# Two-head state matmuls, and a third of one product's transposes moved from TensorE to the sync queue's DMA

## The chip, the cores and the metric

The kernel runs on one core of a Trainium2 chip. A core has engines that run beside each other, each through its own instructions in order: TensorE (PE, matmuls; the profile shows its weight loads apart as PEld), VectorE (DVE), ScalarE (ACT), GpSimd (POOL) and SyncE (SP), which here issues transfers only. Matmul results land in PSUM; the other data lies in SBUF. Sixteen DMA engines move data. The metric is device microseconds (us) of one execution.

## The reference

The inputs r, k, v, w have 4 batches, 8 heads, 768 steps and 48 elements. For each batch and head a recurrence with a 48x48 state runs over the steps:

```python
cur   = einsum(u * k_t, v_t)              # outer product, weighted by u
y_t   = einsum(r_t, state + cur)
state = w_t[:, None] * state + einsum(k_t, v_t)
```

The rows y (3072 rows of 8 x 48 = 384) then go through a mixture of low-rank adapters: eight gate logits by a 384x8 matrix, the two largest kept, softmax over these, and

```python
delta[mask] += weight * ((x[mask] @ A[e]) @ B[e])   # A: 384x16, B: 16x384, 8 adapters
out = x + delta
```

## The kernel before

The 3072 rows are cut into 24 tiles of 128 steps; six tiles (one batch) form a sequence, after which the state begins anew (`t % 6 == 0`). Within a tile the recurrence is done by matmuls, and between tiles by a state that TensorE accumulates.

The stages of one tile `t`, with the line of the profile at which each shows:

- `ln` (L324/L326, ACT): logarithm of w. `cs` (L333, L334, PE) sums it over the steps into `cs_ps`; `grow` (L346, ACT) is its exponential; `ci` (L351, PE) adds the tile's own step, `exps` (L356, ACT) is the inverse exponential. `mult` (L362, DVE) multiplies r and k with these into `rk2`, whose head slots are 64 wide (48 used).
- `tr` (L404, PE) transposes `rk2` in eight pieces, `trev` moves the result to SBUF (ACT at L206 or DVE at L208). `amm` (L442, PE) forms the scores of the eight heads, `aev` (L453, DVE) masks them.
- `rkp` (L379, POOL) is the plain product r*k. For the diagonal term, the sum over u*r*k, it must be transposed: `xk` (L538, PE) transposes three blocks of `rkp` of the tile LEAD = 3 ahead together with three blocks of its own result `xs`, and `xkev` (L206/L208, ACT or DVE) moves all six to SBUF. `dgmm` (L383, PE) multiplies by u, `dgev` (L200/L202) moves the sums of two tiles at a time, and `dv` (L396, POOL) multiplies v by them.
- `kv` (L475, PE) adds the tile's k x v to the state in PSUM: eight matmuls, one for each head, into the diagonal blocks `S_acc[g*64:..., p, g]`. A zeroing matmul (L471) stands ahead of a sequence's first and in the last tile. `sev` (L200 on ACT, L202 on DVE) copies the state to SBUF. The off-diagonal blocks are zero, as only the zeroing matmul writes them.
- `yi` (L498, PE; not in a sequence's first tile) multiplies r by the copied state of the tile before, in four matmuls for two heads each, of 96 columns: so the off-diagonal blocks must be zero. `ya` (L524, PE) adds scores times v. `xev` (L529, DVE) adds `dv`: the result `xs`.
- The adapters: `lgmm` (L559, PE) the logits; then for batches of 4, 4, 4, 4, 4, 2, 1 and 1 tiles `gate` (L566), `gmax` (L573), `gden` (L579, L580), `gsel` (L592/L589), `gmul` (L599, L600, POOL), `zmm` (L607, PE), `zw` (L614, DVE), `zT` (L624, PE), `zTev`. `dmm` (L640, PE) is the second adapter matrix. The last addition `oev` is either on DVE (L651), or on ACT (L649) after an identity matmul (L639, PE) that adds `xs` in PSUM; tiles 22 and 23 use L646 on DVE. `store` (L655, SP) writes the tile.

Loads: w on SP (`load_w`, L255); r and k together, cast to 16 bits on the way by POOL's queue (`load_rk`, L264; the first four tiles plain on SP, L261); v likewise (`load_v`, L276 and L272).

The order of the work is a list written out, `ORDER`: items such as `xk.12` are emitted one after the other, and each engine (SP's and POOL's queues among them) runs its own in that order. An item starts when its engine has come to it, its inputs are there, and its buffer is free. `ENGINES` names for each stage the tiles that go to ACT ('A') or DVE ('D'). Where a product on POOL (`rkp`, `dv`) follows a multiply on DVE in the list, a wait keeps it behind that multiply. `rkp` has three buffers, `S_sb` three, `res` sixteen.

Of the kernel before, what the change touches and what calls it, by code (L numbers as in the profile page):

```python
# [55 lines left out]
ENGINES = {'out': {0: 'A', 3: 'A', 8: 'A', 12: 'A', 13: 'A', 15: 'A', 16: 'A', 18: 'A', 20: 'A', 21: 'A', 17: 'A'},
    'k_id16': {0: 'A'}, 'trev': {0: 'D', 5: 'D', 9: 'D'}, 'xkev': {-3: 'D', -2: 'D'}, 'sev': {0: 'D'}, 'dgev': {1:
    'D', 5: 'D'}, 'cast_v': {1: 'D'}, 'cast_b': {0: 'D'}, 'zTev': {3: 'A', 7: 'A', 11: 'A', 15: 'A', 19: 'A', 21: 'A',
    22: 'A', 23: 'A'}}
# [5 lines left out]
m_zeros.0 load_w.0 load_w.1 szero.0 warm.0 warm.1 warm.2 ln.0 load_rk.0 k_incl.0 k_ident.0 k_strict.0 k_id16.0 warm.3
load_w.2 m_pad.2 cs.0 m_pad.0 grow.0 ln.1 multr.0 k_rest.0 load_rk.1 csx.0 exps.0 multk.0 rkp.0 warm.4 load_rk.4 ci.0
cs.1 warm.5 m_pad.1 m_pad.3 warm.6 warm.7 warm.8 grow.1 ci.1 exps.1 tr.0 trev.0 ln.2 load_v.0 xk.-3 load_v.2 xkev.-3
warm.9 cs.2 grow.2 amm.0 load_rk.6 rkp.1 cast_v.0 ci.2 exps.2 mult.1 tr.1 load_rk.2 rkp.2 trev.1 warm.10 cs.3 xk.-2
load_k.0 aev.0 cast_k.0 load_w.4 grow.3 xkev.-2 ln.4 amm.1 ya.0 dgmm.0 xk.-1 warm.11 load_v.4 dgmm.1 ci.3 exps.3
load_rk.3 mult.2 load_v.6 tr.2 load_v.1 cs.4 xkev.-1 dgev.1 dv.0 kv.0 trev.2 aev.1 mult.3 load_rk.8 sev.0 grow.4 xev.0  # L70
load_v.8 amm.2 rkp.3 ci.4 exps.4 cast_v.1 tr.3 load_w.6 mult.4 aev.2 yi.1 cs.5 dv.1 xk.0 trev.3 grow.5 xkev.0 kv.1
ci.5 ya.1 dgmm.2 ln.6 exps.5 lgmm.0 tr.4 dgmm.3 sev.1 rkp.4 amm.3 xev.1 dgev.3 dv.2 dv.3 rkp.5 load_rk.10 trev.4
mult.5 cs.6 xk.1 kv.2 yi.2 aev.3 load_w.8 tr.5 grow.6 sev.2 xkev.1 ci.6 exps.6 trev.5 ln.8 ya.2 kv.3 amm.4 xev.2 rkp.6
mult.6 dgmm.4 cs.7 yi.3 lgmm.1 ya.3 grow.7 xev.3 xk.2 ci.7 sev.3 tr.6 yi.4 aev.4 exps.7 xkev.2 xk.3 cs.8 dgmm.5 kv.4
xkev.3 mult.7 amm.5 grow.8 dgev.5 aev.5 lgmm.2 trev.6 lgmm.3 gate.3 ci.8 gmax.3 gsel.3 load_rk.12 gden.3 zmm.3 exps.8
sev.4 load_v.12 ya.4 cs.9 tr.7 rkp.7 load_b.0 dv.4 xev.4 gmul.3 load_w.10 kv.6 ln.10 grow.9 trev.7 zw.3 dv.5 amm.6
ci.9 dgmm.6 yi.5 xk.4 zT.3 exps.9 sev.6 cast_b.0 xkev.4 mult.8 cs.10 rkp.8 aev.6 mult.9 zTev.3 kv.7 ya.5 dgmm.7
grow.10 sev.7 dgev.7 tr.8 dmm.2 ci.10 trev.8 ya.6 load_w.12 amm.7 kv.8 xev.5 xk.5 exps.10 cs.11 tr.9 sev.8 xkev.5 yi.7
oev.2 lgmm.4 aev.7 yi.8 grow.11 ln.12 dv.6 dv.7 xev.6 ci.11 dgmm.8 store.2 rkp.9 mult.10 kv.9 exps.11 xk.6 ya.7
load_w.14 cs.12 amm.8 trev.9 xkev.6 dgmm.9 dmm.0 grow.12 dgev.9 xev.7 aev.8 ci.12 sev.9 rkp.10 exps.12 xk.7 xkev.7  # L80
tr.10 trev.10 dv.8 lgmm.6 load_rk.14 cs.13 mult.11 mult.12 rkp.11 ya.8 xev.8 oev.0 kv.10 grow.13 amm.9 aev.9 tr.11
ln.14 ci.13 lgmm.5 dgmm.10 dv.9 load_rk.16 lgmm.7 dmm.1 xk.8 gate.7 exps.13 load_w.16 oev.1 xkev.8 gmax.7 trev.11
load_rk.18 mult.13 amm.10 yi.9 cs.14 gsel.7 grow.14 dgmm.11 zmm.7 dgev.11 gden.7 aev.10 tr.12 ci.14 ya.9 sev.10 kv.12
gmul.7 zw.7 amm.11 dv.10 yi.10 ya.10 rkp.12 zT.7 trev.12 exps.14 cs.15 load_w.18 xev.9 ln.16 xk.9 aev.11 zTev.7 dv.11
rkp.13 sev.12 grow.15 yi.11 tr.13 ya.11 ci.15 xkev.9 trev.13 xev.10 mult.14 load_v.16 rkp.15 rkp.14 amm.12 kv.13 xk.10
dmm.4 exps.15 xev.11 sev.13 xkev.10 aev.12 cs.16 lgmm.8 tr.14 dgmm.12 dmm.5 dmm.7 lgmm.10 dgmm.13 grow.16 oev.4
trev.14 ci.16 mult.15 dgev.13 exps.16 ln.18 load_rk.20 oev.7 oev.5 dv.12 dmm.3 kv.14 amm.13 aev.13 rkp.17 xk.11 ya.12
sev.14 cs.17 xkev.11 xev.12 load_w.20 grow.17 tr.15 dgmm.14 lgmm.9 amm.14 kv.15 dv.13 oev.3 mult.16 ci.17 aev.14
trev.15 exps.17 rkp.16 xk.12 dmm.6 yi.13 lgmm.11 ya.13 mult.17 cs.18 xev.13 rkp.18 gate.11 xkev.12 tr.16 dgmm.15
grow.18 oev.6 gmax.11 amm.15 lgmm.12 trev.16 ci.18 dgev.15 dv.14 xk.13 exps.18 xkev.13 aev.15 yi.14 tr.17 ya.14 cs.19  # L90
store.3 yi.15 amm.16 zmm.11 sev.15 gsel.11 grow.19 trev.17 xev.14 ci.19 mult.18 xk.14 ln.20 tr.18 dgmm.16 ya.15
gden.11 load_w.22 exps.19 cs.20 xkev.14 dgmm.17 gmul.11 dv.15 dgev.17 yi.16 aev.16 load_rk.22 grow.20 trev.18 ya.16
mult.19 zw.11 kv.16 amm.17 store.1 zT.11 xev.15 ci.20 xk.15 dv.16 load_v.20 sev.16 exps.20 tr.19 cs.21 aev.17 rkp.19
zTev.11 xkev.15 grow.21 xev.16 dmm.8 dmm.11 amm.18 oev.8 mult.20 oev.11 lgmm.15 xk.16 yi.17 lgmm.13 lgmm.14 trev.19
gate.15 ci.21 dmm.9 ya.17 store.0 store.6 aev.18 gmax.15 kv.18 dv.17 xkev.16 xev.17 exps.21 amm.19 gsel.15 rkp.20
ln.22 ya.18 gden.15 oev.9 dgmm.19 dgmm.18 xk.17 store.7 store.4 store.5 dgev.19 sev.18 cs.22 gmul.15 xkev.17 dv.18
tr.20 grow.22 aev.19 zmm.15 yi.19 trev.20 lgmm.17 ci.22 ya.19 dv.19 rkp.21 exps.22 kv.19 xev.18 zw.15 sev.19 amm.20
store.11 store.8 zT.15 xev.19 cs.23 zTev.15 mult.21 dmm.10 store.9 dmm.13 rkp.22 oev.13 aev.20 xk.18 xkev.18 dgmm.20
tr.21 trev.21 xk.19 lgmm.16 mult.22 dmm.14 dgmm.21 oev.10 kv.20 xkev.19 rkp.23 dgev.21 amm.21 dmm.12 dv.20 lgmm.18
lgmm.19 yi.20 oev.14 grow.23 sev.20 gate.19 store.10 store.14 oev.12 aev.21 ya.20 dmm.15 ci.23 tr.22 exps.23 trev.22  # L100
gmax.19 yi.21 xev.20 gden.19 ya.21 xk.20 kv.21 dv.21 amm.22 mult.23 tr.23 store.13 store.12 oev.15 xkev.20 sev.21
gsel.19 zmm.19 gmul.19 trev.23 xev.21 store.15 dgmm.23 dgmm.22 xk.21 dgev.23 aev.22 xkev.21 amm.23 kv.22 sev.22 zw.19
zT.19 dv.22 yi.22 ya.22 dv.23 zTev.19 aev.23 xev.22 lgmm.20 lgmm.21 dmm.17 yi.23 ya.23 gate.21 gmax.21 oev.17 store.17
xk.22 xev.23 dmm.18 xkev.22 gsel.21 oev.18 dmm.19 zmm.21 gden.21 kv.23 lgmm.22 store.18 oev.19 store.19 xk.23 gmul.21
# [29 lines left out]
def kernel(  # L134
# [47 lines left out]
    Ss = [const.tile([128, P, 2, D], BF16, name=f"S_{i}") for i in range(S_BUFS)] if KV128 else []  # L182
    rk2s = [const.tile([L, 2, P, 2, 64], BF16, name=f"rk2_{i}") for i in range(NRK)]

    cs_ps = pp.tile([L, 512], F32, name="cs_ps")
# [305 lines left out]
        copy(engine("sev", t), sb, S_acc)  # L491
        st[t]["S"] = sb

    def yi(t):
        d = st[t]
        y_ps = pp.tile([L, H, D], F32, name="y_ps", **slot("y", t))
        for p in range(P):
            nc.tensor.matmul(y_ps[:, 2 * p:2 * p + 2, :].rearrange("s a b -> s (a b)"),  # L498
                             lhsT=d["rkT"][:, 0, p, :],
                             rhs=st[t - 1]["S"][:, p].rearrange("s a b -> s (a b)"),  # L500
                             start=(p == 0), stop=False, skip_group_check=True)
# [30 lines left out]

    def xk(t):
        xk_ps = pp.tile([128, 6, 128], FP16, name="xk_ps", **slot("xk", t))
        for q, src in enumerate((st[t]["xs"] if t >= 0 else None, st[t + LEAD]["rkp"] if t + LEAD < NT else None)):
            if src is not None:
                for j in range(3):
                    nc.tensor.transpose(xk_ps[:, 3 * q + j, :], src[:, j * 128:(j + 1) * 128], ident16)  # L538
# [175 lines left out]
```

## Time and profile before

| | us |
|---|---|
| median of 3 runs (lowest to highest) | 85.75 (85.69 to 86.84) |
| the profiled execution | 85.72 |
| its span in the trace | 84.0 |

The mean granted TensorE clock over the span is 0.984. Busy time over the span: PE 91%, DVE 88%, ACT 82%, POOL 67%. The first 10 us are loading and the first tiles; the last `xev` starts at 75.46 us; what follows is the gates, adapters and stores of the last tiles.

A group's line gives: source line, engine, operation, tiles written and read, shapes and types, count; then total busy us and the mean ns of one; then the idle time of that engine just before them, and who ended it. In the chain and the timelines the first number is the start in us from the span's begin, the second the length. In a wait line stand the total us, how often, and the longest. In a table by stretches each engine has busy us and its count of instructions.

### The profile page before, as it was taken

How to read it: one execution, taken by the hardware profiler on the slowest of the kernel's cores; microseconds unless marked ns; L12 is line 12 of the kernel's file. 1: busy time of each engine (PE TensorE's matmuls, PEld its weight loads, DVE VectorE, ACT ScalarE, POOL GpSimd, SP SyncE). 2: the span in 40 equal slices, each digit the busy share in tenths (PEclk: the TensorE clock that was granted, in tenths of full speed). 3: DMA queues.
4: the chain of work that ended last, by engine and by line, in shares of the span. 5: the costliest groups of instructions: out<-in, count | busy, mean ns of one | idle time of the engine just before them, and what ended most of it. 6: DMA issues, size and time to landing. Idle time of an engine off the chain costs nothing.

```text
span 84.0 us, 3311 instructions
## 1 busy us (share of the span) xinstructions
PE 76.6 (91%) x1322; PEld 58.4 (69%) x1322; DVE 74.2 (88%) x157; ACT 68.9 (82%) x167; POOL 55.9 (67%) x89
## 2 busy tenths in 40 slices
...
GB/s 20 280 335 362 391 374 265 289 252 287 270 225 211 214 216 240 297 274 249 177 192 149 145 190 128 377 303 108 126 202 228 14 96 255 125 12 145 233 316 59
DMA packets 8943, 18.12 MB, mean 216 GB/s; under 512 B 992, under 2 KB 5216, under 8 KB 8928
## 3 DMA queue, kind: packets, MB, share of 16 engines
...
q8 instruction: 10, 0.16, 0.8%
...
## 4 chain that ended last, share of the span: by engine, by line
PE 72%; DVE 15%; DMA 5%; issue 2%; SPq 1%; ACT 1%; ACTq 0%; DVEq 0%
PE trp L404 11%; PE xk_ps L538 9%; PE a_ps L442 8%; DVE rk L362 6%; PE y_ps L524 6%; PE s_ps L475 5%; DMA rk_first<-in_rk_dram 5%; PE d_ps L640 5%; PE z_ps L607 4%; PE y_ps L498 4%; PE cs_ps L351 4%; PE cs_ps L334 4%; PE cs_ps L333 3%; DVE at L453 3%; PE d_ps L639 2%; PE s_ps L559 2%
## 5 line engine op out<-in xcount | busy, mean ns | idle before, releaser
L453 DVE TENSOR_TENSOR at<-a_ps,strict 128x1024 f16<-128x1024 f32 x24 | 29.1, 1214 | 0.3
L379 POOL TENSOR_TENSOR rkp<-rk 128x384 f16<-128x384 f16 x20 | 18.2, 912 | 5.2 <-DVE rk L362 2.7
L396 POOL TENSOR_TENSOR dv<-v,dg 128x384 f32<-128x384 f16 x22 | 18.2, 835 | 3.7 <-ACT dg L200 3.0
L404 PE MATMUL trp<-ident,rk 128*128 128x128 bf16 x192 | 14.7, 219 | 0.5 <-DVE rk L362 0.5
L206 ACT COPY rkT<-trp 128x512 f32<-128x512 f32 x21 | 12.6, 600 | 1.2 <-PE trp L404 1.2
L404 PEld LDWEIGHTS <-rk 128*128 128x128 bf16 x192 | 11.7, 98 | 2.7 <-DVE rk L362 1.5
L346 ACT ACTIVATE e<-cs_ps 128x384 bf16<-128x384 f32 x24 | 12.0, 501 | 1.6 <-PE cs_ps L334 1.6
L529 DVE TENSOR_TENSOR xs<-dv,y_ps 128x384 f16<-128x384 f32 x24 | 13.1, 544 | 0.3 <-PE y_ps L524 0.2
L356 ACT ACTIVATE e<-cs_ps 128x384 bf16<-128x384 f32 x23 | 11.4, 497 | 1.8 <-PE cs_ps L351 1.7
L206 ACT COPY xkT<-xk_ps 128x384 f32<-128x384 f32 (+1 forms) x25 | 11.5, 462 | 0.4 <-PE xk_ps L538 0.2
L362 DVE TENSOR_TENSOR rk<-rk,e 128x768 bf16<-128x768 f16 x20 | 11.1, 560 | 0.0
L200 ACT CAST S_sb<-s_ps 128x384 bf16<-128x384 f32 x19 | 9.4, 492 | 0.7 <-PE s_ps L475 0.3
L442 PE MATMUL a_ps<-rkT 48*128 48x128 bf16 x192 | 9.5, 219 | 0.1
L324 ACT ACTIVATE logw<-w_in 128x768 f16<-128x768 f32 x11 | 9.3, 847 | 0.0
L334 PE MATMUL cs_ps<-logw,strict 128*128 128x384 f16 x24 | 8.2, 340 | 0.4 <-ACT logw L326 0.4
L538 PE MATMUL xk_ps<-ident,rkp 128*128 128x128 f16 x72 | 8.0, 219 | 0.4 <-POOL rkp L379 0.4
L351 PE MATMUL cs_ps<-logw,ident 128*128 128x384 f16 x24 | 8.0, 333 | 0.2 <-ACT e L346 0.2
L524 PE MATMUL y_ps<-v,at 128*128 128x48 f16 x176 | 8.0, 183 | 0.0
L538 PE MATMUL xk_ps<-ident,xs 128*128 128x128 f16 x72 | 8.0, 219 | 0.0
L524 PEld LDWEIGHTS <-at 128*128 128x128 f16 x192 | 7.3, 96 | 0.9
L362 DVE TENSOR_TENSOR rk<-rk_first,e 128x768 bf16<-128x768 f32 (+1 forms) x5 | 4.5, 913 | 3.7 <-DMA rk_first<-in_rk_dram 3.7
L640 PE MATMUL d_ps<-Ball,zT 128*128 128x384 f16 x24 | 7.5, 325 | 0.2 <-ACT zT L206 0.2
...
## 6 DMA issues: line engine op xcount, KB each, us to landing
out_dram<-res SPq DMA_DIRECT2D x24, 192.0 KB, 2.6
...
v<-in_v_dram POOLq DMA_DIRECT2D x3, 192.0 KB, 10.6
w_in<-in_w_dram SPq DMA_DIRECT2D x2, 192.0 KB, 2.5
v_first<-in_v_dram SPq DMA_DIRECT2D x2, 192.0 KB, 7.1
```

Source lines behind the costliest of these rows:

```text
L206: nc.scalar.copy(out=out.bitcast(F32), in_=in_.bitcast(F32))
L346: nc.scalar.activation(out=e2[:, 0], in_=cs_ps[:, 0:HD], func=ACT.Exp, **(dict(bias=CENTRE) if CB else {}))
L362: return nc.vector.tensor_mul(rk2[:, lo:hi].rearrange("s m p h d -> s (m p h) d")[:, :, 0:D], st[t]["rk"][:, lo:hi].rearrange("s m (h d) - ...
L379: return nc.gpsimd.tensor_mul(p_, st[t]["rk"][:, 0], st[t]["rk"][:, 1])
L396: return nc.gpsimd.tensor_mul(dv_, st[t]["v16"], st[t]["dg"].rearrange("p (h o) -> p h o", o=1).to_broadcast([L, H, D]))
L404: nc.tensor.transpose(trp[:, m, p, :], rk2[:, m, p, :, :].rearrange("s a b -> s (a b)"), ident)
L442: nc.tensor.matmul(a_ps[:, g, p, :], lhsT=rkT[base:base + D, 1, p, :], rhs=rkT[base:base + D, 0, p, :], start=True, stop=True)
L453: nc.vector.tensor_mul(at, st[t]["a_ps"].rearrange("s g p f -> s (g p) f"), strict.to_broadcast([128, H, 128]))
L524: nc.tensor.matmul(d["y_ps"][:, h, :], lhsT=d["at"][:, g * P + p, :], rhs=d["v16"][:, h, :], start=(c == 0 and h == 0), stop=(h == H - 1), ...
L529: nc.vector.tensor_add(xs, st[t]["dv"].rearrange("p a b -> p (a b)"), st[t]["y_ps"].rearrange("p a b -> p (a b)"))
L538: nc.tensor.transpose(xk_ps[:, 3 * q + j, :], src[:, j * 128:(j + 1) * 128], ident16)
L640: nc.tensor.matmul(d_ps, lhsT=st[t]["zT"], rhs=Ball, start=not by_pe, stop=True)
```

## The change

Three things change together.

1. `KV128` and `ZS` are on. `kv` becomes four matmuls for two heads each, 128 rows of k by 96 columns of v; the first of a sequence starts the accumulation itself, so the zeroing matmul of 384 columns goes, except one of 8 columns in the last tile. The off-diagonal blocks now hold products of one head's k with the other's v; a new stage `zs` sets them to zero in the SBUF copy, with two memsets on POOL, after `sev` and before the next tile's `yi`. It runs 20 times.
2. For tiles 18 to 23 (`DT`) a new stage `dtr` transposes `rkp` from SBUF to SBUF by three DMA transposes on SP's queue; `xk` leaves these blocks out and `xkev` moves three blocks in place of six. The result has three buffers of its own.
3. `ORDER` is a new list, and `ENGINES` is new: `oev` on ACT for 15 tiles (11 before); `trev` on DVE for tile 5 (0, 5 and 9 before); `xkev` on DVE for -3, -2, -1 and 3 (-3 and -2 before); `sev` on DVE for 0, 2 and 4 (0 before); `dgev` on DVE for 1, 5, 7 and 9 (1 and 5 before); `cast_v.0` instead of `cast_v.1` on DVE; `cast_b` on ACT, `k_id16` and `zTev.23` on DVE.

```diff
-KV128 = False
+KV128 = True
+ZS = True
+DT = (18, 19, 20, 21, 22, 23)
+DT1 = False
...
+    def zs(t):
+        nc.gpsimd.memset(st[t]["S"][0:64, :, 1, :], 0.0)
+        nc.gpsimd.memset(st[t]["S"][64:128, :, 0, :], 0.0)
...
     def xk(t):
         xk_ps = pp.tile([128, 6, 128], FP16, name="xk_ps", **slot("xk", t))
-        for q, src in enumerate((st[t]["xs"] if t >= 0 else None, st[t + LEAD]["rkp"] if t + LEAD < NT else None)):
+        bonus = t + LEAD < NT and t + LEAD not in DT
+        for q, src in enumerate((st[t]["xs"] if t >= 0 else None, st[t + LEAD]["rkp"] if bonus else None)):
...
     def xkev(t):
         sb = wk.tile([128, 6, 128], FP16, name="xkT", bufs=XKT_BUFS)
-        lo, hi = (0 if t >= 0 else 3), (6 if t + LEAD < NT else 3)
+        bonus = t + LEAD < NT and t + LEAD not in DT
+        lo, hi = (0 if t >= 0 else 3), (6 if bonus else 3)
...
+    def dtr(t):
+        sb = wk.tile([128, 3, 128], FP16, name="rkpT", bufs=3)
+        nc.sync.dma_start_transpose(out=sb, in_=st[t]["rkp"].rearrange("p (j f) -> p j f", j=3)) if DT1 else None
+        for j in range(0 if DT1 else 3):
+            nc.sync.dma_start_transpose(out=sb[:, j, :], in_=st[t]["rkp"][:, j * 128:(j + 1) * 128])
+        st[t]["rkpT"] = sb
```

The new list around the last transposes, where the sync queue, POOL and PE meet (SP's items here are `store` and `dtr`; POOL's are `rkp`, `dv`, `zs`):

```diff
+ ... dmm.8 rkp.21 mult.21 oev.11 gmax.15 zs.18 zs.16 oev.8 mult.20 ln.22 amm.18 dmm.10 gsel.15 gden.15 oev.10 dtr.21
+aev.18 tr.21 zmm.15 cs.22 dgmm.19 yi.17 ya.17 dmm.9 trev.21 gmul.15 sev.19 dgev.19 grow.22 zw.15 oev.9 amm.19 tr.20 ci.22
+exps.22 dv.17 xev.17 rkp.20 trev.20 dv.18 kv.20 zT.15 zTev.15 ya.18 aev.19 xk.17 dgmm.21 rkp.23 cs.23 grow.23 amm.20
+xev.18 mult.22 aev.20 xk.18 yi.19 sev.20 xkev.17 ya.19 ci.23 xkev.18 exps.23 tr.22 xk.16 zs.19 dmm.13 store.11 dtr.22
+dv.19 dgmm.22 lgmm.17 dtr.20 kv.21 lgmm.18 xev.19 store.10 zs.20 dgmm.20 dtr.23 xk.19 amm.21 xkev.16 xkev.19 oev.13
+dmm.15 dgev.21 trev.22 oev.15 mult.23 dv.20 lgmm.16 yi.20 ya.20 lgmm.19 sev.21 gate.19 tr.23 yi.21 store.9 aev.21 dv.21
+ya.21 dgmm.23 ...
```

More of the change, by code (lines that the diff above doesn't have):

```diff
@@ L52 @@
 SYNC = True
+ZS = True
+TG = ()
+GADD = ()
+RSPLIT = ()
+ASPLIT = ()
+OSPLIT = ()
+OG = False
+DT = (18, 19, 20, 21, 22, 23)
+DT1 = False
 YA = False
@@ L55 @@
 TAG = {('d', 22): 'y', ('d', 23): 'a_ps'}
[L56 to L59, printed above, removed]
+ENGINES = {'out': {3: 'A', 5: 'A', 8: 'A', 9: 'A', 11: 'A', 14: 'A', 10: 'A', 12: 'A', 15: 'A', 17: 'A', 18: 'A', 19:
[3 rows of a table added]
 NWARM = 12
@@ L64 @@
 ORDER = """
[L65 to L104, printed above, removed]
@@ L105 @@
-dmm.16 zw.21 gate.22 xkev.23 gmax.22 zmm.22 zT.21 gsel.22 lgmm.23 zw.22 oev.16 zTev.21 gden.22 gate.23 zT.22 dmm.20
-gmax.23 gsel.23 zTev.22 zmm.23 store.16 dmm.21 zw.23 zT.23 gden.23 oev.20 dmm.22 store.20 oev.22 oev.21 zTev.23
-store.21 store.22 dmm.23 oev.23 store.23
+load_w.0 load_w.1 m_zeros.0 ln.0 warm.0 warm.1 warm.2 warm.3 warm.4 k_ident.0 k_rest.0 warm.5 k_strict.0 cs.0 warm.6
+load_rk.0 m_pad.3 m_pad.2 m_pad.1 k_id16.0 ln.1 k_incl.0 grow.0 ci.0 cs.1 szero.0 csx.0 warm.7 warm.8 load_w.2 warm.9
@@ new lines @@
+m_pad.0 multr.0 rkp.0 exps.0 load_v.2 grow.1 ci.1 load_rk.1 exps.1 load_rk.4 ln.2 load_v.4 multk.0 tr.0 mult.1 trev.0
+cs.2 amm.0 load_v.0 load_rk.2 aev.0 grow.2 cast_v.0 load_rk.6 rkp.1 ci.2 tr.1 load_v.6 load_w.4 exps.2 mult.2
+load_rk.8 trev.1 xk.-3 cs.3 warm.10 grow.3 amm.1 load_rk.3 load_k.0 kv.0 ci.3 xk.-2 tr.2 ln.4 exps.3 cs.4 aev.1 trev.2
+load_v.1 grow.4 xkev.-2 amm.2 ya.0 ci.4 rkp.2 cast_k.0 exps.4 xkev.-3 sev.0 dgmm.1 dgmm.0 rkp.3 load_v.8 mult.3 dgev.1
+cast_v.1 cs.5 load_rk.10 load_w.6 load_w.8 warm.11 tr.3 xk.-1 zs.0 dv.0 aev.2 dv.1 grow.5 xev.0 mult.4 ci.5 kv.1 yi.1
@@ new lines @@
+ya.1 trev.3 sev.1 amm.3 kv.2 exps.5 sev.2 xk.0 ln.6 tr.4 kv.3 zs.1 zs.2 load_w.10 mult.5 xkev.0 xkev.-1 cs.6 dgmm.2
+trev.4 dgmm.3 yi.2 yi.3 grow.6 ci.6 rkp.5 dgev.3 sev.3 ya.2 tr.5 xev.1 aev.3 kv.4 dv.2 xev.2 rkp.4 exps.6 cs.7 dv.3
+amm.4 xk.1 ln.8 grow.7 ci.7 sev.4 load_rk.12 xk.2 zs.4 zs.3 trev.5 exps.7 xkev.1 rkp.6 mult.6 load_w.12 cs.8 mult.7
+aev.4 xkev.2 grow.8 lgmm.0 ya.3 dgmm.4 lgmm.1 tr.6 dgmm.5 dgev.5 dv.4 dv.5 ci.8 ln.10 xev.3 exps.8 yi.5 rkp.7 amm.5
+aev.5 trev.6 kv.6 sev.6 yi.4 load_rk.18 zs.6 cs.9 xk.3 ya.4 xev.4 load_w.14 grow.9 ln.12 kv.7 tr.7 ci.9 xkev.3 lgmm.2
@@ new lines @@
+amm.6 exps.9 xk.4 cs.10 trev.7 xkev.4 mult.8 tr.8 dgmm.6 lgmm.4 ya.5 grow.10 aev.6 rkp.9 mult.9 ci.10 dgmm.7
+load_rk.14 dgev.7 ln.14 amm.7 lgmm.3 exps.10 rkp.8 trev.8 ya.6 gate.3 xev.5 yi.7 dv.6 aev.7 dv.7 sev.7 load_v.12 cs.11
+grow.11 load_rk.22 xk.5 xkev.5 tr.9 zs.7 kv.8 sev.8 load_b.0 ci.11 ya.7 amm.8 exps.11 xev.6 gmax.3 xev.7 gsel.3
+mult.10 xk.6 trev.9 kv.9 cs.12 sev.9 zmm.3 grow.12 rkp.10 tr.10 ci.12 yi.8 mult.11 dgmm.8 gden.3 xkev.6 lgmm.6 kv.10
+dgmm.9 exps.12 xk.7 aev.8 dgev.9 trev.10 xkev.7 gmul.3 zw.3 cs.13 grow.13 amm.9 lgmm.7 ya.8 zT.3 ci.13 cast_b.0 rkp.11
@@ new lines @@
+zs.8 dv.8 mult.12 zs.9 lgmm.5 tr.11 aev.9 yi.9 rkp.12 zTev.3 dmm.0 exps.13 cs.14 dgmm.10 dv.9 trev.11 xev.8 rkp.18
+load_w.16 ln.16 amm.10 oev.0 ya.9 xk.8 load_w.18 tr.12 grow.14 ci.14 aev.10 dmm.3 gate.7 xkev.8 sev.10 exps.14 amm.11
+xev.9 gmax.7 trev.12 yi.10 zs.10 load_rk.16 dgmm.11 cs.15 mult.13 oev.3 mult.14 gsel.7 grow.15 aev.11 dgev.11 dv.10
+ya.10 xk.9 xkev.9 tr.13 ci.15 exps.15 xev.10 gden.7 ln.18 trev.13 dmm.1 oev.1 zmm.7 lgmm.9 cs.16 kv.12 dgmm.12 store.0
+rkp.13 grow.16 sev.12 mult.15 amm.12 xk.10 yi.11 xkev.10 gmul.7 load_v.16 ci.16 exps.16 tr.14 kv.13 zw.7 dv.11 zT.7
@@ new lines @@
+zTev.7 lgmm.10 dmm.2 rkp.14 ya.11 aev.12 xev.11 dgmm.13 dgev.13 sev.13 cs.17 rkp.19 trev.14 grow.17 store.1 dv.12
+amm.13 dmm.6 zs.13 xk.11 zs.12 kv.14 oev.2 dmm.5 dtr.18 ci.17 tr.15 xkev.11 load_w.20 sev.14 exps.17 aev.13 oev.5
+rkp.15 mult.16 ya.12 kv.15 lgmm.11 lgmm.8 cs.18 grow.18 amm.14 yi.13 xev.12 oev.6 gate.11 trev.15 ya.13 dmm.4 ci.18
+exps.18 load_rk.20 dgmm.14 xk.12 xkev.12 mult.17 aev.14 tr.16 cs.19 dv.13 dgmm.15 trev.16 amm.15 sev.15 rkp.22 xev.13
+dgev.15 dmm.7 oev.4 rkp.16 gmax.11 yi.14 oev.7 tr.17 aev.15 dv.14 kv.16 ya.14 xev.14 xk.13 grow.19 ln.20 ci.19 exps.19
@@ new lines @@
+xkev.13 sev.16 trev.17 rkp.17 zmm.11 zs.14 amm.16 mult.18 aev.16 gsel.11 dv.15 store.5 cs.20 store.2 store.4 store.6
+grow.20 xk.14 dgmm.18 yi.15 tr.18 gden.11 xkev.14 ci.20 ya.15 dgmm.16 amm.17 kv.18 load_w.22 exps.20 trev.18 dtr.19
+lgmm.14 dgmm.17 xev.15 mult.19 dgev.17 cs.21 sev.18 gmul.11 xk.15 zs.15 load_v.20 xkev.15 yi.16 ya.16 lgmm.13 zw.11
+kv.19 lgmm.15 lgmm.12 zT.11 store.3 grow.21 dv.16 aev.17 zTev.11 xev.16 ci.21 tr.19 exps.21 gate.15 trev.19 dmm.11
+dmm.8 rkp.21 mult.21 oev.11 gmax.15 zs.18 zs.16 oev.8 mult.20 ln.22 amm.18 dmm.10 gsel.15 gden.15 oev.10 dtr.21 aev.18
@@ new lines @@
+tr.21 zmm.15 cs.22 dgmm.19 yi.17 ya.17 dmm.9 trev.21 gmul.15 sev.19 dgev.19 grow.22 zw.15 oev.9 amm.19 tr.20 ci.22
+exps.22 dv.17 xev.17 rkp.20 trev.20 dv.18 kv.20 zT.15 zTev.15 ya.18 aev.19 xk.17 dgmm.21 rkp.23 cs.23 grow.23 amm.20
+xev.18 mult.22 aev.20 xk.18 yi.19 sev.20 xkev.17 ya.19 ci.23 xkev.18 exps.23 tr.22 xk.16 zs.19 dmm.13 store.11 dtr.22
+dv.19 dgmm.22 lgmm.17 dtr.20 kv.21 lgmm.18 xev.19 store.10 zs.20 dgmm.20 dtr.23 xk.19 amm.21 xkev.16 xkev.19 oev.13
+dmm.15 dgev.21 trev.22 oev.15 mult.23 dv.20 lgmm.16 yi.20 ya.20 lgmm.19 sev.21 gate.19 tr.23 yi.21 store.9 aev.21
```

11 lines of the change are left out of this document (9 added, 2 removed), and 3 rows, old and new, of the table ENGINES.

## The prediction

> **What bounds the kernel now.** I read the page first (engine totals), then busy time by stretches of the span, then the chain that ended last, then the groups by form. The profiled execution took 85.72 us, 84.0 of it span, so 1.72 us lie around the span; the median of the runs is 85.75, and I work against 85.72.
>
> ```profile
> PE 76.6 (91%) x1322; PEld 58.4 (69%) x1322; DVE 74.2 (88%) x157; ACT 68.9 (82%) x167; POOL 55.9 (67%) x89
> ```
>
> ```profile
> core 0: us, PE busy (x) PEld busy (x) DVE busy (x) ACT busy (x) POOL busy (x), PEclk, DMA share, GB/s
> 10.00:50.00 40.00, 39.47 (x740) 31.42 (x741) 39.16 (x73) 37.66 (x89) 33.87 (x47) 1.00 1.03 240
> 50.00:70.00 20.00, 20.00 (x388) 16.54 (x385) 19.86 (x47) 17.46 (x46) 14.44 (x21) 1.00 0.67 172
> ```
>
> From 10 to 70 us VectorE (DVE) is busy 59.02 of 60 us and TensorE (PE) 59.47. The two are bounds together. PE's busy time by itself proves little, as its ends are modelled; the chain of waits does better, since there each group lasts until its successor takes over, and in the middle it runs from one PE group to the next:
>
> ```profile
> 52.01 0.34 PE xk_ps L538 x6
> 52.34 0.17 PE y_ps L498 x4
> 52.51 0.45 PE trp L404 x8
> ```
>
> ```profile
> 61.10 0.17 PE s_ps L471
> 61.27 0.24 PE s_ps L475 x8
> 61.50 0.33 PE a_ps L442 x8
> ```
>
> Those are the real prices on PE: 0.45 us for eight transposes, 0.24 for the eight state matmuls of a tile, 0.17 for four matmuls of 96 columns or for one of 384. ScalarE (ACT) has 2.3 us free in 10 to 50 and 2.5 in 50 to 70. GpSimd (POOL) has 6.13 us free in the first of these stretches and 5.56 in the second. These are what the change spends.
>
> **The change, part by part.**
>
> *State matmuls.* A tile's eight matmuls (L475, 0.24) become four of 96 columns with weights of full width. The four of L498 have just that shape and take 0.17, so 20 tiles (t % 6 < 5) save 20 x 0.07 = 1.4 us of PE. The zeroing matmul L471 ran five times; four go, the last shrinks to 8 columns: 0.7. If full-width weights cost more than L498 shows, the 1.4 falls toward nothing; 1.0 of the total below is then left.
>
> *Transposes.* Tiles 18 to 23 drop 18 of the transposes at L538; six take 0.34, so 18 x 0.057 = 1.0 us of PE goes. Six evictions on ACT shrink to half.
>
> *Moves between engines.* Rows by form:
>
> ```profile
> L651 DVE TENSOR_TENSOR res<-d_ps,xs 128x384 f32<-128x384 f32 x11 | 5.9, 548 | 0.0
> L649 ACT COPY res<-d_ps 128x384 f32<-128x384 f32 x11 | 5.3, 480 | 0.9 <-PE d_ps L640 0.6
> L206 ACT COPY rkT<-trp 128x512 f32<-128x512 f32 x21 | 12.6, 600 | 1.2 <-PE trp L404 1.2
> L208 DVE COPY rkT<-trp 128x1024 bf16<-128x1024 bf16 x3 | 2.0, 661 | 0.0
> L206 ACT COPY xkT<-xk_ps 128x384 f32<-128x384 f32 x21 | 10.3, 489 | 0.2
> L206 ACT COPY xkT<-xk_ps 128x192 f32<-128x192 f32 x4 | 1.3, 317 | 0.2 <-PE xk_ps L538 0.2
> L208 DVE COPY xkT<-xk_ps 128x384 f16<-128x384 f16 x2 | 0.7, 351 | 0.3 <-PE xk_ps L538 0.3
> L200 ACT CAST S_sb<-s_ps 128x384 bf16<-128x384 f32 x19 | 9.4, 492 | 0.7 <-PE s_ps L475 0.3 <-PE s_ps L559 0.3
> L202 DVE CAST S_sb<-s_ps 128x384 bf16<-128x384 f32 x1 | 0.5, 547 | 0.0
> L202 DVE COPY dg<-s_ps 128x16 f32<-128x16 f32 x2 | 0.3, 170 | 0.0
> L202 DVE CAST Ball<-Ball_f 128x384 f16<-128x384 f32 x1 | 0.4, 360 | 0.0
> L200 ACT CAST ident<-ident 128x128 f16<-128x128 bf16 x1 | 0.3, 282 | 0.0
> L206 ACT COPY zT<-zT_ps 128x64 f32<-128x64 f32 x2 | 0.4, 215 | 0.1
> ```
>
> DVE: four final adds leave (4 x 0.548 = -2.19), two `trev` leave (-1.32), `cast_b` leaves (-0.36); two `sev` arrive (+1.09), two `dgev` (+0.34), `xkev.-1` (+0.35), `xkev.3` with twice the width (estimate 0.5, between 0.351 and the 0.661 of the wider copy), `k_id16` and `zTev.23` (estimates 0.28 and 0.2, from ACT's 0.282 and 0.215). Sum -1.1 us. ACT: +4 x 0.480 + 2 x 0.600 - 2 x 0.492 - 0.317 - 0.489 - 6 x (0.489 - 0.317) and the small ones: within 0.2 of zero. PE gains four identity matmuls (L639, one of 384 columns each, 0.17): +0.7. PE in all: -1.4 - 0.7 - 1.0 + 0.7 = -2.4.
>
> So the two bounds fall unequally, and DVE's smaller fall counts: **at most 1.1 us, if nothing else is late**. Nor can the new order itself win much in the middle: DVE's idle time in 10 to 70 us is 0.98. In the last 8 us, a line of small steps, I see no row that moves it; I put it at nothing, with 0.7 us either way.
>
> *Zeroing on POOL (`zs`).* New: 40 memsets of 64 partitions x 4 x 48 bf16, two after each of 20 evictions. Before, POOL held only `rkp`, `dv`, small gate products and load issues:
>
> ```profile
> L379 POOL TENSOR_TENSOR rkp<-rk 128x384 f16<-128x384 f16 x20 | 18.2, 912 | 5.2 <-DVE rk L362 2.7 <-PE cs_ps L334 1.5 <-PE cs_ps L351 0.5
> masks.py:65 POOL MEMSET strict<- 128x128 f16 x1 | 0.2, 204 | 0.0
> L698 POOL MEMSET const-uint8-127<- 128x1 uint8 x1 | 0.1, 101 | 0.0
> ```
>
> Between one and 128 elements a memset grows by 103 ns, 0.81 ns each, so 192 elements give 101 + 155 = 0.26 us, a pair 0.51 (my value, nearest in kind). From below: two at 0.10 each, 0.2 a pair. From above: the per-element price of `rkp`, 912/384 = 2.4 ns, which makes 0.46 each and 0.91 a pair. The work added is 20 x 0.51 = 10 us. Where it falls decides:
>
> ```profile
> core 0: us, DVE busy (x), PEclk, DMA share, GB/s
> 10.00:50.00 40.00, 7.08 (x13) 1.00 1.03 240
> ```
>
> That is `xev` (L529): 13 tiles pass in 10 to 50 us. The new order has 12 `zs` up to `xev.13`, so 12 x 0.51 = 6.1 us meet 6.13 us of free time. POOL would be full there, with no room for its own waits, and it has some that no order removes wholly:
>
> ```profile
> POOL rkp L379 <- DVE rk L362: 6.8, 5, 4.2
> POOL dv L396 <- ACT dg L200: 3.0, 5, 1.3
> ```
>
> A `zs` also waits: for the eviction `sev`, on ACT or DVE. Queued behind it on POOL stand `rkp` (awaited by PE in `xk`), `dv` (awaited by DVE in `xev`) and the next cast loads. And `yi` of the next tile, which needed only the eviction, now needs POOL too. In the old order POOL ran so far ahead that no wait in the list names `dv` as its cause. I charge **+0.7 us**; from nothing (POOL runs without a gap) to +4.8 (a pair at 0.91: 12 x 0.40 over what is free).
>
> *Transposes on the sync queue (`dtr`).* Eighteen issues on SP, three for a tile; no row shows this operation. The nearest are plain transfers from SP: how long an issue holds the queue, and how long until it lands.
>
> ```profile
> 5.49 0.56 SPq L261 DMA_DIRECT2D rk_first<-in_rk_dram  x1
> 4.78 0.67 SPq L255 DMA_DIRECT2D w_in<-in_w_dram  x1
> 31.00 0.35 SPq L655 DMA_DIRECT2D out_dram<-res  x1
> ```
>
> ```profile
> out_dram<-res SPq DMA_DIRECT2D x24, 192.0 KB, 2.6
> w_in<-in_w_dram SPq DMA_DIRECT2D x2, 192.0 KB, 2.5
> Ball_f<-in_moe_B_dram SPq DMA_DIRECT2D x1, 192.0 KB, 12.0
> ```
>
> Three issues at 0.35 to 0.67 plus 2.5 for the last to land: 3.6 to 4.5 us from product to use, estimate 4.0. Tile 18's product is made long before its `dgmm`; tile 20 is the tight one. Between `rkp.20` and `dgmm.20` PE has `kv` two times, `ya` two, `amm.20`, `tr.22`, `zT.15`, `yi.19`, `cs.23`, `ci.23`, `xk` three, a `dmm` and four small products: by the prices above about 3.5 us, less 0.9 for `rkp` itself: 2.6. So it would come some 1.4 us late, with PE standing in front of `dgmm.20`. PE's surplus over DVE (2.4 against 1.1) eats about half: **+0.7**; from nothing (issues end early, POOL made `rkp.20` early) to +8, if a landing takes the 12.0 of `Ball_f` (9.5 later) and PE's 1.3 of spare is all that absorbs it. That far end I hold unlikely: `Ball_f` travelled among the first loads, in the stretch whose DMA share is 1.03, and from 50 to 70 us the share is 0.67. The stores behind `dtr` on SP have sixteen result buffers and wait unharmed. If cover fails there, a store held behind a transpose late in the run costs its own delay at the end.
>
> On this the Trainium skill speaks against the change: the page "VectorE: DVE Perf Modes", section "The three transpose paths", lists 1309 ns for a 128x128 transpose by DMA and 390 ns by TensorE. By that figure three in a row would take 3.9 us, about what the sum has; no run here shows it yet, and PE's row of 0.34 for six is already well below its own figure.
>
> *Sum:* 85.72 - 1.1 + 0.7 + 0.7 = **86.0 us**, no change that a measurement of this kernel can tell (about 2%: 84.0 to 87.5).
>
> **The rivals.**
>
> *POOL becomes the bound (slower).* One mechanism, in 10 to 50 us: a `zs` pair above 0.51 us leaves POOL more than it can do. For: POOL is full by the sum already. Against: `rkp` of later tiles can be moved about, and after 50 us there is room. At 0.7 a pair it is 12 x 0.19 = 2.3, plus 1 to 2 us of waits, less DVE's 1.1: 88 to 89; at 0.91 about 90.
>
> *The transposes come late (slower).* Tiles 21, 22, 20 and 23 follow on each other on SP. Their twelve issues at 0.67 take 8 us and 2.5 to land; PE has some 9 us of work from `rkp.21` to `dgmm.23`. Of these, 0.9 go to `rkp.21` itself, so 8.6 are to be met. It decides from about 0.8 us an issue: twelve then take 9.6, come 3.5 late, 2.2 after PE's spare of 1.3, on 85.3 (the sum without its term for the transposes): 87.5. At 1.0 it is 89.9. For it: a transpose is a longer instruction for the queue than a copy may be. Against: every issue in the rows is below 0.7, and SP has little else to do. By the 1309 ns of the Trainium skill ("VectorE: DVE Perf Modes", "The three transpose paths"), taken as time in which the queue does nothing else, the twelve would take 15.7 us and the time would be near 93; no run here shows that yet.
>
> *Both are covered (faster).* The order hides `zs` and `dtr`, and DVE's 1.1 us come out, with up to 1 us of its idle time and some of the tail: 83.2 to 84.0. For it: PE is 2.4 us lighter, so DVE would be fed earlier. Against: DVE keeps all but 1.1 of its 74.2 us.
>
> *The state matmuls get no shorter.* Then PE falls by 1.0 only, still about as much as DVE: inside the forecast.
>
> **How the numbers follow.** Forecast 0.47 (84.0 to 87.5, its sum 86.0); POOL the bound 0.20; late transposes 0.16; faster 0.17. The case on the fast side reaches to 83.2, the two slow ones to 90; leaving out about 1 in 10 on each side gives 83.5 to 89.5. Faster by over 2%: 0.17; within: 0.47; slower: 0.36.
>
> **What would show it.** Right: L462 in groups of four near 0.17 and no full-width L471; DVE's total near 73; POOL near 66 busy and over 38 of 40 us in 10 to 50; `zs` memsets near 0.26; the landing of a transpose 2.5 us or more after its issue, and a PE wait before `dgmm` on a DMA around tiles 20 to 23. Wrong: memsets near 0.1 or above 0.4; waits of DVE for `dv` in the middle that sum to several us; a transpose issue far from 0.35 to 0.67; or a tail after the last `xev` more than 1 us from today's.

## The result, and the profile after

The changed kernel takes 99.5 us in the median of four runs (98.19 to 99.84), against 85.77 for the kernel before: a ratio of 1.147, interval 1.129 to 1.166. That is 13.7 us slower, and outside the range that was given. The profiled execution is one of the longer ones, 99.81 us with a span of 97.8. (What moved to the DMA is a quarter of the product's transposes, 18 of 72, not a third.)

The page of the changed kernel, engine totals, answers first:

```profile
PE 79.3 (81%) x1224; PEld 59.5 (61%) x1224; DVE 73.8 (75%) x158; ACT 69.0 (71%) x166; POOL 65.5 (67%) x129
```

The work itself came out about as summed: DVE 73.8 (74.2 before), POOL 65.5 (55.9 before), ACT unchanged. No engine has 13 us more to do. So the time went into waiting. PE's total rose though it has fewer matmuls, because part of them ran at a lower granted clock (last section). The waits of the changed kernel (total us, how often, longest) name what for:

```profile
POOL dv L406 <- ACT dg L210: 8.2, 2, 8.0
PEld L393 <- DMA rkpT<-rkp: 7.1, 7, 1.2
PE s_ps L393 <- DMA rkpT<-rkp: 6.3, 7, 1.2
...
POOL rkp L389 <- DMA rkpT<-rkp: 3.2, 2, 2.9
```

L393 is `dgmm`; its input `rkpT` is what the sync queue's transposes write. The chain that ended last, from 72.5 us on, shows the larger stall piece by piece (start, length):

```profile
72.50 0.20 PE y_ps L538 x8
72.69 0.18 PE cs_ps L361
72.88 0.35 SPq L569
73.23 0.05 issue
73.28 1.23 SPq L569
...
74.56 1.22 SPq L569
75.78 0.05 issue
...
75.89 1.17 SPq L569
...
77.10 1.23 SPq L569
...
78.38 1.23 SPq L569
...
79.71 0.52 SPq L678
80.23 0.05 issue
...
80.34 1.09 SPq L569
81.44 0.05 issue
81.49 1.22 SPq L569
82.71 0.05 issue
82.76 2.32 DMA rkpT<-rkp
...
85.13 0.18 PE s_ps L393
```

For 12 us the chain leaves PE and runs on the sync queue's own instruction stream (SPq): one issue of a DMA transpose behind the other, 1.1 to 1.23 us each, and the last lands 2.32 us after its issue began. PE's `dgmm` of tiles 22, 20 and 23 take their blocks one at a time as they arrive. By stretches, with the granted clock:

```profile
72.90:85.10 12.20, 5.89 (x81) 4.36 (x78) 4.54 (x11) 3.40 (x10) 3.10 (x7) 0.72 0.16 39
```

All engines are less than half busy (PE 5.89 of 12.2), the DMA engines carry 39 GB/s, and the clock granted to PE is 0.72 in the mean. The transposes are slow to be issued, not to be moved. The same line's group, `dtr`:

```profile
L569 SPq DMA_TRANSPOSE rkpT<-rkp x18: 1093/1230/2676, 46.4 to 82.8; - x18
...
DMA to landing us min/median/max: 2.2/2.4/7.0
```

Another stall, of some 3 us, lies earlier in the chain:

```profile
49.63 4.23 DMA rkpT<-rkp
...
54.02 0.92 POOL rkp L389
...
54.99 0.35 PE xk_ps L553 x3
```

Here POOL could not begin a product because its buffer, one of three, was still being read by the transposes of tile 18, the first of which needed 7.0 us to land. PE stood before `xk` for that product.

### The profile page after: what moved, and what is told of

Read it like the earlier page. It is cut to its first block, busy times and chain, and to the rows that moved or that the text cites. A ratio compares the mean times of both kernels' runs of the same rounds, so it can differ in the third digit from the quotient of the medians.

```text
span 97.8 us, 3190 instructions
## 1 busy us (share of the span) xinstructions
PE 79.3 (81%) x1224; PEld 59.5 (61%) x1224; DVE 73.8 (75%) x158; ACT 69.0 (71%) x166; POOL 65.5 (67%) x129
## 3 DMA queue, kind: packets, MB, share of 16 engines
q1 hardware_dynamic: 9360, 12.42, 37.9%
## 4 chain that ended last, share of the span: by engine, by line
POOL 27%; PE 25%; DMA 21%; SPq 12%; issue 5%; DVE 4%; DVEq 1%; ACT 1%; POOLq 0%; ACTq 0%
SPq L569 11%; POOL rkp L389 11%; DMA rk<-in_rk_dram 10%; POOL dv L406 9%; DMA rkpT<-rkp 7%; DMA rk_first<-in_rk_dram 4%; PE trp L414 3%; PE z_ps L630 3%; PE xk_ps L553 3%; PE a_ps L452 2%; POOL rk L274 2%; PE d_ps L663 2%; PE y_ps L538 2%; PE d_ps L662 2%; DVE rk L372 2%
## 5 line engine op out<-in xcount | busy, mean ns | idle before, releaser
L216 ACT COPY xkT<-xk_ps 128x384 f32<-128x384 f32 (+1 forms) x23 | 9.5, 422 | 10.6 <-PE xk_ps L553 10.5
L414 PE MATMUL trp<-ident,rk 128*128 128x128 bf16 x192 | 15.5, 226 | 0.9 <-DVE rk L372 0.9
L216 ACT COPY rkT<-trp 128x512 f32<-128x512 f32 x23 | 13.7, 593 | 1.7 <-PE trp L414 1.7
L414 PEld LDWEIGHTS <-rk 128*128 128x128 bf16 x192 | 12.5, 101 | 2.9 <-DVE rk L372 1.8
L452 PEld LDWEIGHTS <-rkT 48*128 48x128 bf16 x192 | 5.7, 95 | 5.9 <-issue 2.8
L210 ACT CAST S_sb<-s_ps 128x384 bf16<-128x384 f32 x17 | 8.3, 491 | 0.7 <-PE s_ps L472 0.4
L553 PE MATMUL xk_ps<-ident,rkp 128*128 128x128 f16 x54 | 6.2, 225 | 2.5 <-POOL rkp L389 2.5
L663 PE MATMUL d_ps<-Ball,zT 128*128 128x384 f16 x24 | 8.1, 336 | 0.2 <-DVE zT L218 0.2
L672 ACT COPY res<-d_ps 128x384 f32<-128x384 f32 x15 | 7.2, 500 | 1.1 <-PE d_ps L663 0.9
```

What stands on the lines that cost most here:

```text
L216: nc.scalar.copy(out=out.bitcast(F32), in_=in_.bitcast(F32))
L414: nc.tensor.transpose(trp[:, m, p, :], rk2[:, m, p, :, :].rearrange("s a b -> s (a b)"), ident)
L452: nc.tensor.matmul(a_ps[:, g, p, :], lhsT=rkT[base:base + D, 1, p, :], rhs=rkT[base:base + D, 0, p, :], start=True, stop=True)
```

## The experiments

Fifteen kernels were run. Ratios are to the kernel before, run on the same chip beside them; its median there was 85.98 to 86.37 us.

**Transposes back on TensorE** (`no_dt`).

```diff
     def dtr(t):
-        sb = wk.tile([128, 3, 128], FP16, name="rkpT", bufs=3)
-            nc.sync.dma_start_transpose(...)
+        dt_ps = pp.tile([128, 3, 128], FP16, name="dt_ps", **slot("dt", t))
+        for j in range(3):
+            nc.tensor.transpose(dt_ps[:, j, :], st[t]["rkp"][:, j * 128:(j + 1) * 128], ident16)
+    def dtrev(t):   # ScalarE copies dt_ps to rkpT
```

(The cut is abridged. The same edit gives `rkp` six buffers and finds places in the list for the new items.)

> The changed kernel with the six transposes back on TensorE (three transposes and one ScalarE copy for a tile, at free places of the order near the old ones, six buffers for rkp); state matmuls, zeroing on GpSimd, the new order and the moves between engines stay. Theory (each DMA transpose holds the sync queue for 1.2 us; what follows from that is the whole loss): 84.5 to 87 us, no wait on a DMA before dgmm. Rival (GpSimd, full since the zeroing came, or the new order, costs a good part too): over 88 us, with waits of VectorE for dv that sum to over 3 us.

89.37 us, ratio 1.039 (1.029 to 1.048). Ten of the 13.7 us go with the DMA transposes, and no wait names them any longer; but 3 us stay, over what the theory gave. The waits of DVE for `dv`, by which the rival was to show, sum to 0.6 us only. Neither side had it right whole.

**Only the transposes, in the old order** (`before_dt`).

> The kernel before with only the DMA transposes of tiles 18 to 23, each issued right behind its product in the old order. Theory: in the old order the last six products end at about 52, 59, 61, 65, 67 and 68.5 us, the queue needs 3.7 us for each and 2.4 to land, so the last lands at about 80 where its use stood at 72.7: 91 to 95 us. Rival (the queue is late only because the new order puts the transposes behind stores and close to their use): 85 to 88 us.

100.22 us, ratio 1.165 (1.157 to 1.173). The transposes alone, with nothing else changed, lose as much as the whole change, and more than the 91 to 95 expected. PE waited 11.4 us before `dgmm`, 5.1 at the longest:

```profile
PE s_ps L385 <- DMA rkpT<-rkp: 11.4, 5, 5.1
```

**Only the two-head matmuls and the zeroing, in the old order** (`before_kv`, `before_kv2`). In the first each `zs` stands right behind its `sev` in the list; in the second half way to its use.

> The kernel before with only the two-head state matmuls and the zeroing on GpSimd, each zeroing right behind its eviction in the old order. Theory (a pair of memsets is 0.51 us and just fits in GpSimd's free time): 85 to 87.5 us. Rival (GpSimd becomes the bound): over 88 us, GpSimd at 39 of 40 us from 10 to 50 us and VectorE waiting for dv. If TensorE alone were the bound: 83.5 to 84.5.

102.34 us (100.08 to 104.24; no interval came out). Not the amount, it seems, but the place: POOL stood before the memsets until ACT had done the eviction just ahead of them in the list, and with it stood the products queued behind. The waits of that kernel:

```profile
POOL S_sb L497 <- ACT S_sb L202: 11.6, 8, 2.5
...
PEld L544 <- POOL rkp L381: 6.5, 6, 1.9
...
DVE xs L535 <- POOL dv L398: 5.1, 4, 2.2
```

> As before_kv, but each zeroing stands in the list half way between its eviction and its use. In before_kv GpSimd stood 11.6 us before memsets, waiting for the eviction just ahead. Theory (that was place, not amount): 86 to 89 us, GpSimd's wait for the evictions under 4 us. Rival (amount: the old order cannot carry 10 us more on GpSimd wherever they stand): over 95.

93.3 us, ratio 1.087 (1.078 to 1.097). The wait for the eviction is gone from the list of waits and 9 us with it; now PE waits for the memsets instead:

```profile
PE y_ps L504 <- POOL S_sb L498: 3.8, 5, 1.8
```

Theory and rival both missed the number; that place decides much of it is shown, that a good place in the old order exists is not.

**One instruction for three blocks** (`dt1`): `DT1 = True`, one DMA transpose of 128x384 in place of three of 128x128.

> The changed kernel with one DMA transpose for the three blocks of a tile in place of three. If the price is one of the instruction, six take the queue 7 to 8 us in place of 22, and the time is 86 to 90 us. If it is one of the blocks, each takes some 3.7 us and the time stays at 97 to 100.

89.38 us, ratio 1.039 (1.029 to 1.048) in two runs. The group by itself settles what a transpose costs:

```profile
L567 SPq DMA_TRANSPOSE rkpT<-rkp x6: 1184/1186/1602, 46.7 to 70.2; - x6
...
DMA to landing us min/median/max: 2.3/3.0/6.3
...
  POOL rkp L389: 1.7, 1
```

Three blocks in one instruction hold the queue for 1.19 us in the median, one block for 1.23: **the price is of the instruction**, not of its blocks. (In `dt1_bufs` below, the six took 1.18 to 2.20 us, 1.48 in the median: still far from the 3.7 of three instructions.) The bytes are the same (12.41 and 12.42 MB on the queues that hold them). What waits for `rkpT` is now POOL alone, once, for a buffer.

**More buffers** (`bufs`, `dt1_bufs`): `RKP_BUFS = 6`, in the changed kernel and in `dt1`.

> The changed kernel with six buffers for rkp in place of three. In the changed kernel's trace GpSimd stood 3.2 us because rkp waited for transposes that still read its buffer, from 51 to 54 us above all. Theory (two stalls, this and the one before dgmm from 73 to 85 us, which add up): 95.5 to 97.5 us, the later stall as long as before. Rival (the first stall is hidden, since the queue is late in any case): 98.5 to 100.

95.17 us, ratio 1.108 (1.103 to 1.113): the earlier stall was worth 3.4 us by the two ratios and was not hidden by the later one, where PE still waited 4.9 us:

```profile
PE s_ps L393 <- DMA rkpT<-rkp: 4.9, 6, 1.2
```

> The changed kernel with one DMA transpose for a tile and six buffers for rkp. In dt1's trace GpSimd stood 1.7 us, and everything behind it, for a buffer that the first transpose still read: that one took 6.3 us to land. Theory (with this gone, the transposes cost nothing, and what is left is not theirs): 87 to 88.5 us. Rival (the stall only hid other waits): 89 to 90.

86.67 us in eleven runs, ratio 1.0045 (0.9996 to 1.0094). With six instructions and six buffers **the loss is gone**, but for what the interval leaves (up to 0.9%); that is a little more than the theory gave. In its trace nothing waits for a transpose. All other parts of the change are still in this kernel: two-head matmuls, zeroing on POOL, new order, moves between engines.

**No zeroing, and the order alone** (`no_zs`, `order_only`). `no_zs` is `no_dt` without the memsets; it leaves the other heads' blocks in the state, so only its time is of use. `order_only` takes the old state matmuls in addition.

> As no_dt (transposes on TensorE, new order), but the 40 zeroing memsets are left out; so the state's other-head blocks enter yi, and only the time is of use. Theory now (the 3 us by which no_dt is slower than the kernel before are GpSimd's: it is filled by the memsets and everybody waits a little): 84.5 to 86.5 us, GpSimd near 33 of 40 us from 10 to 50. Rival (the new order itself, or its moves between engines, costs the 3 us): 88 to 89.5.

88.91 us, ratio 1.033 (1.027 to 1.039), against 1.039 (1.029 to 1.048) with them. Ten us less on POOL gained nothing that these intervals tell apart. The theory that the 3 us of `no_dt` are the memsets' falls.

> As no_zs (transposes on TensorE, no zeroing), with the old state matmuls too: of the change only the new order and the moves between engines are left. Theory (the order itself loses the 3 us, at the start and around tiles 11 to 14, whatever GpSimd does): 88 to 90.5 us. Rival (the loss is the two-head form's, with its zeroing and its waits): 85 to 87 us.

91.39 us, ratio 1.062 (1.053 to 1.070). Against `no_zs` only the state matmuls differ: 2.5 us, where the prediction's PE prices (1.4 and 0.7) gave 2.1. The time is above the range of its theory (88 to 90.5): the new order by itself loses even more than that, so it needs the lighter PE.

**Earlier load, earlier issue** (`dt1_load`, `early`, `early_noload`). In `dt1_load` one cast load goes ahead of another in POOL's queue; in the others every transpose is issued behind its product and the next w load, ahead of the stores.

> As dt1_bufs, with the cast load of r and k of tiles 4 and 5 moved ahead of that of v of tiles 2 and 3 in GpSimd's queue, as in the old order. Theory (the new order's later start, 1 to 2 us by the fifth masked score, comes from this load, which took 10.8 us to land in no_zs): 0.7 to 1.5 us under dt1_bufs. Rival (the start is late for other reasons): within 0.4 us of dt1_bufs.

87.19 us, ratio 1.015 (1.008 to 1.021): no gain over `dt1_bufs` (86.67), so moving this load earlier gains nothing that shows.

> As dt1_load, with each DMA transpose issued as soon as the sync queue can (behind its product and the next w load, ahead of the stores) and six buffers for its result. Theory (late landing behind other traffic still costs a little): 85.5 to 87.5 us, no wait on a transpose. Rival (nothing more to win there): as dt1_load, within 0.5.

87.04 us, ratio 1.013 (1.007 to 1.020): the rival; nothing more to win there.

> As early18 with one DMA transpose for a tile (six of them). early was the same but for an earlier load of r and k, which dt1_load did not gain from. If dt1_bufs still loses to late landings: 85.3 to 86.3 us. If the transposes in dt1_bufs are hidden wholly: 86.4 to 87.2.

87.2 us, ratio 1.014 (1.005 to 1.023): the upper end of the second range. No engine waits for a transpose in it, as in `dt1_bufs`: there too they are hidden.

**Eighteen transposes, but early** (`early18`): as `early_noload`, with three instructions for a tile.

> The changed kernel with its 18 DMA transposes, six buffers for rkp and for the result, and each transpose issued as soon as the queue can (behind its product and the next w load, ahead of the stores). If what counts is 1.23 us of the sync queue for each instruction (22 us in all, begun some 5 to 10 us sooner): the last still come some 4 to 6 us late: 89.5 to 93 us, between bufs (95.2) and dt1_bufs (86.7). If the place in the queue alone was at fault: 86 to 88.

90.52 us, ratio 1.047 (1.033 to 1.061), as expected from 22 us of queue that begins sooner: PE still waits 2.4 us for them, and 3.3 us more than with six at the same places are lost, which is the price of the number of instructions there. Earlier places, together with six buffers for the result in place of three, account for another part (95.2 to 90.5 against `bufs`); the two were not tried apart.

**Six transposes in the old order** (`before_dt1`, `before_dt1e`).

> As before_dt, but one DMA transpose for a tile's three blocks. Theory (the price is that of the instruction on the sync queue, 1.2 to 1.3 us): six of them keep pace with products that come 2 to 7 us apart; 85 to 86.5 us, TensorE 1 us lighter, VectorE as full as before. Rival (the transposes also land late): 87 to 92, with waits of TensorE for them.

91.06 us, ratio 1.061 (1.058 to 1.065): the rival. Its chain has one long piece:

```profile
58.39 0.94 POOL rkp L381
...
59.34 6.04 DMA rkpT<-rkp
...
65.43 0.32 PE s_ps L385 x6
...
66.73 0.85 PE trp L406 x8
```

The product of tile 19 is ready at 59.3, its transpose issued at once, and it lands 6.0 us later, in a stretch (60 to 65 us) in which the DMA engines are full:

```profile
55.00:60.00 5.00, 5.00 (x92) 3.88 (x90) 5.00 (x9) 4.44 (x13) 3.97 (x7) 1.00 0.89 209
60.00:65.00 5.00, 2.21 (x51) 1.65 (x51) 4.06 (x12) 2.08 (x6) 2.07 (x4) 0.88 1.08 149
65.00:70.00 5.00, 4.57 (x53) 4.00 (x55) 1.24 (x2) 2.23 (x6) 2.48 (x3) 0.50 0.88 199
```

The last three numbers are granted clock, DMA share and GB/s: a share of 1.08 while PE waits, and a clock of 0.50 behind the wait. There eight transposes of `tr` take 0.85 us in the chain, where they took 0.45 in the kernel before.

> As before_dt1 (old order, old state matmuls, one DMA transpose for each of tiles 18 to 23), with the product and transpose of tile 19 moved right behind those of tile 18 and six buffers. In before_dt1 the transpose of tile 19 was issued at 59.3 us and landed 6.0 us later, beside a full load of other traffic, and TensorE stood 3.2 us before dgmm. If that landing was all of its loss of 5 us: 85 to 86.5 us. If six transposes disturb other transfers too: 87 to 90.

88.54 us (86.84 to 89.41; no interval came out): half of the loss by the median, most of it by the shortest run. In the trace, taken at 88.7 us with a span 3.0 us longer than before, PE waits only 1.1 us for transposes, one of which stands behind three stores in the queue. DVE's wait for the first loads (`rk_first`), ahead of any transpose, is 5.8 us, against 3.7 in the trace before. This wait runs from 1.9 to 5.8 us over the traces of this case, so how much of the rest belongs to the transposes stays open.

## Why the prediction was wrong, point by point

**The step that failed is "Transposes on the sync queue", its price of an issue.** I took 0.35 to 0.67 us from plain transfers on the same queue as the nearest rows, and counted 3.6 to 4.5 us from product to use. The landing was right (2.5 taken, 2.4 median, both counted from the start of the issue, so that my sum holds the last issue twice). The issue was not: 1.23 us, outside both ends of my range, so three take 3.7 and eighteen 22. The sum for tile 20 also took the queue as free when `rkp.20` is ready. In the list `dtr.22` stands ahead of `dtr.20`, and the queue of the changed kernel was taken without a gap from `rkp.21` on:

```profile
66.07 3.75 SPq L569 DMA_TRANSPOSE rkpT<-rkp  x3
69.93 0.53 SPq L678 DMA_DIRECT2D out_dram<-res  x1
70.55 9.06 SPq L569 DMA_TRANSPOSE rkpT<-rkp  x6
79.71 0.52 SPq L678 DMA_DIRECT2D out_dram<-res  x1
80.34 3.64 SPq L569 DMA_TRANSPOSE rkpT<-rkp  x3
```

These are tiles 21, then 22 and 20 together, then 23. POOL made `rkp.20` by 70.0 us, and its first transpose was issued at 75.9. At 0.35 to 0.67 us an issue the twelve would hold the queue for 4 to 8 us; as it was, they and the two stores held it for 18. I had the mechanism as the second rival, with its point of decision at 0.8 us an issue and 89.9 at 1.0; continued to 1.23 by the same sum (14.8 us for twelve, 2.5 to land, 8.6 to meet them and 1.3 of spare) it gives 92.7. It had 0.16 of chance. Of the 6.8 us between that and 99.5, 3.4 belong to the earlier stall (next point); the rest was not taken apart. Two sums of this step don't come out as written: its far end is +9.6 by its own terms (1.4 + 9.5 - 1.3), not +8, and the second rival at 15.7 us of queue comes to 93.6. The Trainium skill's 1309 ns ("VectorE: DVE Perf Modes", "The three transpose paths") is for a 128x128 transpose, and the queue's 1.23 us is close to it; I let it stand as a price for the landing path, beside a range of plain copies, when it was the only row for the operation itself. But where that page's figure is read as one for each 128x128 block, the six instructions of three blocks, 1.19 us each, contradict it: here it is one for each instruction.

**A wait was left out of that step.** I named the stores behind `dtr` as the ones to wait. What waited was POOL, in front: `rkp` has three buffers, and here a buffer that a DMA read was held until the transfer had landed (`rkp` waited 2.9 us for it, from 51 to 54 us). This cost 3.4 us (`bufs`) and, with six instructions, 2.7 (`dt1` to `dt1_bufs`). The long end of landing, 12 us from `Ball_f`, which I called unlikely, did not occur, but the longest landing of each kernel with DMA transposes was 5.3 to 7.9 us, and once was enough.

**Zeroing on POOL.** The price was right, by the changed kernel's groups of instructions (busy us, mean ns of one, idle time ahead of it and what ended it):

```profile
L505 POOL MEMSET S_sb<- 64x192 bf16 x20 | 5.1, 257 | 2.1 <-DVE S_sb L212 1.0 <-ACT S_sb L210 1.0
...
L506 POOL MEMSET S_sb<- 64x192 bf16 x20 | 5.1, 253 | 1.0
```

By stretches (busy time of PE, PEld, DVE, ACT and POOL, then granted clock, DMA share and GB/s):

```profile
10.00:50.00 40.00, 37.07 (x648) 29.45 (x647) 37.75 (x72) 36.27 (x83) 37.14 (x66) 1.00 0.99 236
```

A pair takes 0.51 us, just what was taken; POOL is busy 37.1 of 40 us in 10 to 50, where I said over 38. As a bound it did not show: without the memsets (`no_zs`) the time was the same within the intervals. The charge of 0.7 us on this head is not supported, and the price of a pair that the first rival needed did not come. The memsets were left out only with the transposes on TensorE; in the changed kernel itself the chain runs on POOL, products and memsets, for most of 20 to 47 us, and what the memsets cost there is not known.

**State matmuls, moves, engine totals.** Right in size: the full-width L471 is gone, `kv` takes 0.17 to 0.19 us in several pieces of the chain (0.28 in others, at full clock too), the pair of experiments gave 2.5 us for 2.1, and DVE's total fell to 73.8, by less than the 1.1 taken.

**DVE's relief as the gain.** The sum without its term for the transposes was 85.3; the kernel that has none of their cost, `dt1_bufs`, is at 1.0045 of before, 86.1 on the profiled execution's scale. So the relief did not arrive. In `early_noload`, 0.5 to 2.3% over before, with no wait for a transpose, the stretches read, in the same columns,

```profile
10.00:50.00 40.00, 37.25 (x651) 29.55 (x648) 37.74 (x73) 36.21 (x83) 37.39 (x67) 1.00 0.99 234
50.00:70.00 20.00, 19.73 (x374) 16.22 (x373) 19.88 (x43) 18.28 (x48) 17.94 (x37) 1.00 0.82 164
```

DVE is busy 57.6 of 60 us where it had been 59.0, PE 57.0 where it had been 59.5: the work that left turned into idle time, most of it in 10 to 50 us (for DVE 1.4 us more than before in this stretch, 0.8 of them in 10 to 20). That the new order could win little was right; that it could lose in the middle had no term in the sum. Which waits make it up was not settled.

**What I had left out of the gain.** The same order with TensorE's transposes and six extra ScalarE copies (`no_dt`) runs at 1.039, with six DMA transposes (`dt1_bufs`) at 1.0045. Moved well, the transposes are thus worth 2 to 3 us here, where I counted 1.0 us of PE and ACT's smaller copies as nothing. Part of it may be my placing of those copies.
